# The second MLP of an attention and two-MLP kernel in five token chunks instead of six, with part of its weights streamed

## The chip, the cores and the metric

The kernel runs on one core of one Trainium2 chip. The metric is the device time of one execution in microseconds: before the change 1404.86 us, the median of 3 runs (1404.59 to 1405.29).

## The reference, cut to what matters

Attention (8 batches of 576 tokens, so 4608 tokens in all) gives 512 features per token, a gated MLP follows (hidden width 1536), and then the second MLP, which alone is touched here:

```
h = x @ w_in            # x 4608 x 512, w_in 512 x 2048
g = h * cos(h)
out = g @ w_out         # w_out 2048 x 512
```

All of it is float32. The kernel feeds TensorE with float32r operands, each number split into a high and a low part, and makes three passes (high by high, high by low, low by high) for every product.

## The kernel before, in words

The tokens of the second MLP are cut into chunks. A chunk has two halves of `TH` = 384 tokens, so that six chunks cover 4608. Both matrix products of a chunk are done by a Strassen-like scheme with seven products in place of eight; the halves are one of the directions that it cuts. Every matmul has a 128x128 weight tile as its stationary operand, and one half (384 columns) of one operand as its moving one.

*Up phase* (`period`, `product`). All six chunks go through the up product first. A chunk has eight periods (`NPF`, the pieces of the hidden width); a period makes the seven products of one piece, six matmuls each. The products are numbered by `n`; the order on TensorE in a period is 0 of this period, 3 and 4 of the one before, 1 of this one, 6 and 5 of the one before, 2 of this one. ScalarE copies sums between the PSUM tiles (`copy`), and with VectorE it makes the cosine of the period before (`phase`, `rest`, `sine`, `times`), which GpSimd's queue stores to `h2` in DRAM (`store_g`). `x_work` fits the next chunk in: its four quadrants `xb` are loaded, VectorE makes four sums `xt` of them, and each of the seven operands is split into high and low (`split_x2`: ScalarE writes the high part, VectorE the low one) into a tile `xs`. The tables `X_SUM`, `X_NEXT` and `X_THIS` say at which place of which period.

*Down phase* (`down_mm` and the loop at the end). Chunk after chunk, seven products of 48 matmuls each (`ORDER`); the operands are read back from `h2` (`load_g`, tiles `raw2`), combined by VectorE (`sums2`), split (`prep2`), and the results are evicted, transposed and stored (`evict2`, `finish_out`). The first chunk's operands are prepared in the last periods of the up phase (`PREP2`).

*Storage.* Weight pieces of 256 KB (`up`, `wd`) live in 56 slots (areas `U_AREAS`), which hold all 56 up pieces; as the last chunk's up products finish with them, the slots take 48 of the 56 down pieces (eight slots are left for partial sums). Only the down pieces of products 4 and 2 take turns in one set of slots (`RING`). The `xs` tiles have 9 buffers, the tiles called `x` (loads, sums, cosines) 16. A tile is taken when its code line is reached; the instruction that first writes it waits on the chip until the last reader of the slot's former tile is done.

*What sets the order.* The order on each engine is the one in which the code is written (a manual schedule); there is no planner. Loads go out on SyncE's queue (SP), which issues them in code order: a load whose slot is not free yet holds back every load behind it, but SP runs ahead of the other engines as far as slots allow.

Of the kernel before, what the change touches and what calls it, by code (L numbers as in the profile page):

```python
# [30 lines left out]
TH = 384  # L31
NCH = NT // (2 * TH)
# [11 lines left out]
U_AREAS = (6, 4, 4, 6, 6, 6, 2, 4, 4, 4, 4, 2, 2, 2)  # L44
U_FIRST = (0, 7, 4, 5, 11, 2, 8, 13, 9, 3, 10, 6, 12, 1)
RING = (4, 2)
# [20 lines left out]
def attention_mlp_kernel(ctx: ExitStack, tc: tile.TileContext, qT, kT, vP, pP, wgv, w12, out):  # L67
# [627 lines left out]
    def xt(shape, dt, name):  # L695
        if "m" in late:
            return lt(shape, dt, "x", name, 16)
        x_n[0] += 1
        if x_n[0] <= 4:
            return w2_new(shape, dt, "r" if x_n[0] <= 2 else "p", name)  # L700
        return hr_tile((0, 0) if x_n[0] <= 7 else (0, 1), shape, name)
# [3 lines left out]
    def load_x2(c):  # L705
        for a in range(2):
            for t in range(2):
                xb[a, t] = xt([128, 2, TH], F32, "xb")
                r0 = 2 * TH * c + TH * t
                SP.dma_start(out=xb[a, t], in_=x2d[2 * a:2 * a + 2, :, r0:r0 + TH].rearrange("k p n -> p k n"))  # L710

    def sum_x2(key, x, y):
        xb[key] = xt([128, 2, TH], F32, "xt")
        DVE.tensor_tensor(out=xb[key], in0=xb[x], in1=xb[y], op=ALU.subtract)
# [8 lines left out]
    def new_xs():  # L723
        return late["x"].tile([128, 2, 2, TH], F32R, tag="xs", name="xs", bufs=9)

    def split_x2(n, to):
        if to[n] is None:
            to[n] = new_xs()
        split(xb.pop(RIGHT[n]), to[n][:, 0], to[n][:, 1])

    with tc.manual_schedule():
# [145 lines left out]
        for s_ in range(len(SETS)):  # L877
            end = s_ == len(SETS) - 1
            for i in range(7):
                evict = strassen(s_, i)  # L880
                sums1(s_, i)
                for fp in range(3):
                    prep(*nxt(s_, i), fp)
                if i == 4:
                    load_h(s_ + 1, 0, 0)
                elif i == 5:
                    load_h(s_ + 1, 1, 1)
                    load_h(s_ + 1, 0, 1)
                elif i == 6:
                    load_h(s_ + 1, 1, 0)  # L890
                for _ in range(STEPS_D[s_][i]):
                    w2_step()
                if (s_, i) == (3, 6):
                    w2_flush()
                if end and i == 1:
                    load_x2(0)
                elif end and i == 4:
                    stage["gates"].close()
                    stage["pad"].close()
                    late["x"] = ctx.enter_context(tc.tile_pool(name="xs", bufs=1, side="right", reuse_waits="tile"))  # L900
                    x_now = [new_xs() for _ in range(7)]
# [27 lines left out]
        areas = [a for a in U_FIRST for _ in range(U_AREAS[a])]  # L929

        def load_up(q, n):
            a = tag_of["up", q, n] = areas.pop(0)
            up[q, n] = slots[a].pop(0)
# [5 lines left out]
        def load_wd(n, f):  # L939
# [3 lines left out]
        def vt():  # L943
            return lt([128, 2, TH], F32, "v", "v", 2)

        for q in range(3):
            for n in UP_ORDER:
                load_up(q, n)
# [11 lines left out]
        def bd_tiles():  # L960
            return [pu.tile([128, 512], F32, tag=n, name=n)[:, :TH] for n in ("pb", "pd")]
# [26 lines left out]
        def store_g(p, t, g):  # L988
            c, q = divmod(p, NPF)
            r0 = 2 * TH * c + TH * t  # L990
            nc.gpsimd.dma_start(out=h2[2 * q:2 * q + 2, :, r0:r0 + TH].rearrange("f p n -> p f n"), in_=g)
# [21 lines left out]
        def xt3(name):  # L1013
            return lt([128, 2, TH], F32, "x", name, 16)
# [26 lines left out]
        def down_mm(i, fps, ms_all=((0, 1),)):  # L1041
            n = ORDER[i]
            which = {0: 0, 1: 0, 3: 0, 4: 1, 6: 2, 2: 3, 5: 3}[n]
            first = n in (0, 4, 6, 2)
            if first and 0 in fps:
                if which == 3:
                    acc2[which] = bd_tiles()
                else:
                    o2 = ac_tile("o2")
                    acc2[which] = [o2[:, m, :TH] for m in range(2)]  # L1050
# [18 lines left out]
        def load_g(s_, k, t):  # L1069
            if s_ < NCH:  # L1070
                r0 = 2 * TH * s_ + TH * t
                for fp in range(4):
                    r = raw2[s_, k, t, fp] = xt3("raw2")
                    f0 = NPF * k + 2 * fp
                    SP.dma_start(out=r, in_=h2[f0:f0 + 2, :, r0:r0 + TH].rearrange("f p n -> p f n"))
# [4 lines left out]
        def prep2(s_, n, fp):  # L1080
# [3 lines left out]
            g = g2[n, fp] = new_xs()  # L1084
# [17 lines left out]
        def finish_out(s_, a, t, o_):  # L1102
            ot = lt([128, TH // 32, 2, 32], F32, "v", "ot", 2)
            for m in range(2):
                DVE.transpose(out=ot[:, :, m, :], in_=o_[m])  # L1105
            r0 = 2 * TH * s_ + TH * t
            queues = (nc.gpsimd,) if s_ < NCH - 1 else (SP, ACT) if (a, t) == (1, 0) else (SP,)
            for al in range(4):
                c0 = 128 * al + 64 * a
                queues[al % len(queues)].dma_start(  # L1110
                    out=out[r0:r0 + TH, c0:c0 + 64].rearrange("(b r) d -> r b d", r=32),
# [3 lines left out]
        def evict2(s_, n, acc):  # L1115
            for m in range(2):
                if n in (0, 1, 2, 3):
                    part2[n, m] = ut((n, m), [128, TH], F32, "part")
                    copy(part2[n, m], acc[m])
# [25 lines left out]
        def period(p):  # L1145
            new, old, older = (pairs.get(x) for x in (p, p - 1, p - 2))
            if p <= LAST:
                c, q = divmod(p, NPF)
                if p >= 1 and p + 2 < NPF:
                    for n in UP_ORDER:  # L1150
                        load_up(p + 2, n)
# [3 lines left out]

            def A(x):
                return x["ac"][:, 0, :TH]

            def C(x):
                return x["ac"][:, 1, :TH]  # L1160
# [8 lines left out]
            if older:  # L1169
                older["p"] = xt3("cp")  # L1170
                phase(older["p"], older["ac"][:, :, :TH])
            if p <= LAST and p != 1:
                start(p)
            if old and p != 1:
                product(D_, p - 1, 3, True)
            if p == 0:
                mark(B_, p)
                pairs[1] = {"ac": ac_tile("ac")}
                start(1)
            if p <= LAST:  # L1180
                copy(B_, A(new))
            if older:
                rest(older["p"], older["ac"][:, :, :TH])
                older["s"] = xt3("cs")
                phase(older["s"], older["hs"])
            if old:
                product(A(old), p - 1, 4, False)
                old["hs"] = xt3("hs")
                plus(old["hs"][:, 1], old["v"][:, 1], D_)
# [4 lines left out]
            if p <= LAST:  # L1194
                product(B_, p, 1, False)
            elif old:
                down_mm(0, (0,))
            if old:
                product(D_, p - 1, 6, False)
            if older:  # L1200
                times(older["p"], older["ac"][:, :, :TH])
                store_g(p - 2, 0, older.pop("p"))
                del older["ac"]
            if p <= LAST:
                copy(C(new), B_)
                new["v"] = vt()
                copy(new["v"][:, 0], B_)
            if older:
                sine(older["s"])
            if p > LAST and old:  # L1210
                down_mm(0, (1,))
            if old:
                product(C(old), p - 1, 5, False)
                plus(old["hs"][:, 0], old["v"][:, 0], D_)
# [6 lines left out]
            if p == 0:  # L1221
                product(D_, p, 3, True)
# [17 lines left out]
        for s_ in range(NCH):  # L1240
            for i in range(7):
                n = ORDER[i]
                acc = down_mm(
                    i, (2, 3) if s_ == i == 0 else range(4), ((0,), (1,)) if (s_, i) == (NCH - 1, 6) else ((0, 1),)
                )
                if n in RING:
                    for f in range(NPF):
                        del wd[n, f]
                        ut_done(("wd", n, f))
                    if n == RING[1] and s_ + 1 < NCH or n == RING[0]:  # L1250
                        for f in range(NPF):
                            load_wd(RING[1] if n == RING[0] else RING[0], f)
# [12 lines left out]
                elif i == 6:  # L1265
                    load_g(s_ + 1, 1, 0)
                if s_ or i != 1:
# [46 lines left out]
```

## Time and profile before

| | |
|---|---|
| median of 3 runs | 1404.86 us |
| profiled execution | 1405.46 us, span 1403.7 us |
| TensorE busy | 1387.8 us (99%) |
| VectorE busy | 1130.4 us (81%) |
| ScalarE busy | 829.8 us (59%) |
| DMA | 329.35 MB, mean 235 GB/s |
| the second MLP's matmuls | from 698.4 to 1399.1 us of the span |

PE is TensorE's matmuls, PEld its weight loads, DVE VectorE, ACT ScalarE, POOL GpSimd, SP SyncE; an engine with a q behind it is its DMA queue. The granted TensorE clock is at full speed in all 40 slices of the span. Matmuls are pipelined: the duration of one is longer than the distance from one to the next, and the distance is what the time is made of.

### The profile page before, as it was taken

The page shows a single profiled execution, that of the slowest core. Times are in us where ns is not written, and L with a number is a line of the kernel's source. Part 1 is how long each engine was busy: PE and PEld are TensorE (multiplying, and loading weights), DVE is VectorE, ACT ScalarE, POOL GpSimd, SP SyncE. Part 2 cuts the span into 40 slices and gives each one's busy share as a digit, 9 for nine tenths or more (in the row PEclk, how much of TensorE's full clock was granted, in tenths as well). Part 3 has the DMA queues.
Part 4 walks back from the last instruction along what each step waited for, and adds up shares of the span by engine and source line. Part 5 has one row for each costly group of instructions (what it writes and reads, how often), then busy time and mean ns, then how long its engine had stood idle before and what let it go on. Part 6 is the DMA issues. An engine that isn't in the chain of part 4 may idle for free.

```text
span 1403.7 us, 25278 instructions
## 1 busy us (share of the span) xinstructions
PE 1387.8 (99%) x9644; PEld 1278.5 (91%) x9644; DVE 1130.4 (81%) x1515; ACT 829.8 (59%) x1226; POOL 257.9 (18%) x424
## 2 busy tenths in 40 slices
PE   8999999999999999999999999999999999999998
PEld 6678888888898888898899999999999999999998
DVE  5779889889866898987858778787779788787886
ACT  5866566666644555554558777787775444544443
POOL 1112222222231111121012211212211202112020
PEclk9999999999999999999999999999999999999999
DMA  8947978887698648358494243242798756747641
GB/s 328 408 174 271 356 262 305 311 284 287 248 411 306 233 165 305 137 189 305 146 386 158 108 151 145 115 157 113 270 391 262 272 202 198 251 123 267 207 143 34
DMA packets 148504, 329.35 MB, mean 235 GB/s; under 512 B 21664, under 2 KB 58016, under 8 KB 146976
## 3 DMA queue, kind: packets, MB, share of 16 engines
q1 hardware_dynamic: 110240, 201.95, 41.1%
q0 software_dynamic: 36480, 123.76, 22.5%
q10 hardware_dynamic: 1664, 2.03, 0.4%
q8 instruction: 76, 1.25, 0.4%
q14 instruction: 44, 0.36, 0.1%
HBM read 202.38 MB, written 125.30 MB: 233 GB/s over the span
## 4 chain that ended last, share of the span: by engine, by line
PE 90%; DVE 4%; issue 2%; DMA 2%; ACT 1%; POOL 0%; POOLq 0%; ACTq 0%; SPq 0%; DVEq 0%
PE o L1057 18%; PE o L652 17%; PE ac L971 14%; PE pv L535 7%; PE pg L535 7%; PE pd L971 7%; PE pd L1057 4%; PE pb L1057 4%; PE pb L971 4%; PE wp L495 3%; PE pv L524 2%; PE pg L524 1%; DMA hr<-h 1%; PE pp L234 1%; PE tp L224 1%
## 5 line engine op out<-in xcount | busy, mean ns | idle before, releaser
L652 PE MATMUL o<-g,w 128*128 128x512 f32 (+1 forms) x1260 | 259.7, 368 | 2.2 <-DVE g L112 1.4
L652 PEld LDWEIGHTS o<-g,w 128*128 128x128 f32 x1260 | 219.3, 189 | 42.3 <-DVE g L112 1.9
L1057 PE MATMUL o<-xs,wd 128*128 128x384 f32 x1440 | 251.9, 336 | 0.0
L1057 PEld LDWEIGHTS o<-xs,wd 128*128 128x128 f32 x1440 | 249.8, 188 | 0.0
L971 PE MATMUL ac<-xs,up 128*128 128x384 f32 x1152 | 215.9, 336 | 0.6 <-ACT v L1008 0.6
L971 PEld LDWEIGHTS ac<-xs,up 128*128 128x128 f32 x1152 | 201.1, 188 | 1.0 <-ACT v L1008 0.9
L111 ACT ACTIVATE xs<-raw 128x768 fp32r<-128x768 f32 x168 | 134.0, 845 | 71.8 <-DVE raw L1100 69.0
L112 DVE TENSOR_TENSOR xs<-raw,xs 128x768 fp32r<-128x768 f32 x168 | 149.6, 950 | 23.6 <-ACT xs L111 23.6
L535 PE MATMUL pv<-a,wp 128*128 128x288 f32 x1008 | 150.6, 298 | 3.0 <-DVE h L567 2.8
L535 PEld LDWEIGHTS pg<-a,wp 128*128 128x128 f32 x1008 | 137.7, 188 | 16.8 <-issue 5.7
L111 ACT ACTIVATE g<-hr 128x1024 fp32r<-128x1024 f32 (+1 forms) x105 | 101.3, 977 | 85.1 <-DVE hr L632 34.7
L535 PE MATMUL pg<-a,wp 128*128 128x288 f32 x1008 | 150.3, 298 | 0.4 <-ACT E L208 0.4
L535 PEld LDWEIGHTS pv<-a,wp 128*128 128x128 f32 x1008 | 137.6, 188 | 11.5 <-DVE h L567 5.7
L112 DVE TENSOR_TENSOR g<-hr,g 128x1024 fp32r<-128x1024 f32 (+1 forms) x105 | 113.0, 1113 | 30.9 <-ACT g L111 30.8
L553 ACT ACTIVATE silu<-pg 128x576 f32<-128x576 f32 x96 | 62.5, 652 | 112.8 <-PE pg L535 103.9
L971 PE MATMUL pd<-xs,up 128*128 128x384 f32 x576 | 115.5, 336 | 0.0
L567 DVE TENSOR_TENSOR h<-silu,pv 128x576 f32<-128x576 f32 x96 | 72.1, 751 | 52.2 <-PE pv L535 18.2
L971 PEld LDWEIGHTS pd<-xs,up 128*128 128x128 f32 x576 | 101.0, 188 | 0.2
L568 POOL DMA_DIRECT2D h<-h x96 | 53.2, 554 | 243.3 <-DVE h L567 221.7
L1110 POOL DMA_DIRECT2D out<-ot x80 | 49.4, 620 | 242.5 <-DVE ot L1105 179.0
L1100 DVE TENSOR_TENSOR raw<-raw,raw 128x768 f32<-128x768 f32 x96 | 86.0, 949 | 1.0 <-DMA raw<-h 0.8
L997 DVE SCALAR_TENSOR_TENSOR cp<-ac,cp 128x768 f32<-128x768 f32 x48 | 45.9, 956 | 40.4 <-ACT cp L994 39.6
(132 smaller groups left out, 2070.2 us busy)
## 6 DMA issues: line engine op xcount, KB each, us to landing
raw<-h SPq DMA_DIRECT2D x96, 384.0 KB, 7.1
wd<-w2d SPq DMA_DIRECT2D x136, 256.0 KB, 5.7
h<-h POOLq DMA_DIRECT2D x96, 288.0 KB, 5.3
hr<-h SPq DMA_DIRECT2D x48, 512.0 KB, 7.2
raw<-in_w SPq DMA_DIRECT2D x44, 512.0 KB, 4.8
h<-cp POOLq DMA_DIRECT2D x48, 384.0 KB, 3.1
h<-cs POOLq DMA_DIRECT2D x48, 384.0 KB, 2.8
up<-w2u SPq DMA_DIRECT2D x56, 256.0 KB, 6.7
```

Source lines behind the costliest of these rows:

```text
L111: ACT.activation(out=hi, in_=src, func=AF.Copy)
L112: eng.tensor_tensor(out=lo, in0=src, in1=hi.bitcast(F32), op=ALU.subtract)
L535: PE.matmul(out=p_[:, c, :HS], lhsT=w[:, u, x, o:o + 128], rhs=a2[b][:, u, y, HS * c:HS * c + HS], start=(n == 0), stop=(n == 5),)
L553: ACT.activation(out=s_, in_=pg[:, :, :HS], func=AF.Silu)
L567: DVE.tensor_tensor(out=h_, in0=s_, in1=pv[:, :, :HS], op=ALU.mult)
L568: nc.gpsimd.dma_start(out=h1[f, :, S * b:S * b + S], in_=h_.rearrange("p c n -> p (c n)"))
L652: PE.matmul(out=acc[:, m, :N], lhsT=wd1[n, fp][:, j, 256 * x + 128 * m:256 * x + 128 * m + 128], rhs=g1[n, fp][:, y, j, :], start=(first a ...
L971: PE.matmul(out=out, lhsT=w[:, u, 128 * k:128 * k + 128], rhs=x[:, v, k, :], start=(first and k == 0 and i == 0), stop=(k == 1 and i == 2) ...
L997: DVE.scalar_tensor_tensor(out=out, in0=h_, scalar=1.0 / TWO_PI, in1=out.bitcast(I32), op0=ALU.mult, op1=ALU.subtract)
L1057: PE.matmul(out=acc[m], lhsT=wd[n, 2 * fp + j][:, x, 128 * m:128 * m + 128], rhs=g2[n, fp][:, y, j, :], start=(first and fp + j + q == 0), ...
L1100: DVE.tensor_tensor(out=to, in0=x, in1=y, op=ALU.subtract)
L1110: queues[al % len(queues)].dma_start(out=out[r0:r0 + TH, c0:c0 + 64].rearrange("(b r) d -> r b d", r=32), in_=ot[32 * al:32 * al + 32].rea ...
```

## The change: what it does

The half widths come from a table `TW` with one entry per chunk: two chunks with halves of 480 tokens and three of 448. Every place that had `TH` takes the chunk's width. Tiles have the width of the largest chunk (`xs`: 512), and to hold them 11 of the 56 weight slots go and one of the nine `xs` buffers.

With 45 weight slots, the up pieces of periods 0 to 4 stay resident (`QS` = 5, 35 slots), and the 21 pieces of periods 5 to 7 go through the other ten slots in every chunk. A product that is done with a streamed piece frees the slot and the next streamed piece is loaded (`up_ring`). In the down phase the pieces of products 4, 1, 3 and 5 are streamed (32 of 56 per chunk); 13 of them are loaded ahead of the first chunk. The loads of the down ring now stand behind the chunk's `load_g` calls, at the same place in the loop. The split of the second operand moves from place (6, 2) to (7, 0).

```diff
-TH = 384
-NCH = NT // (2 * TH)
+TW = (480, 480, 448, 448, 448)
+TX = max(TW)
+NCH = len(TW)
+T0 = tuple(2 * sum(TW[:c]) for c in range(NCH))
-RING = (4, 2)
+QS = 5
+RING = (4, 1, 3, 5)
...
-    def new_xs():
-        return late["x"].tile([128, 2, 2, TH], F32R, tag="xs", name="xs", bufs=9)
+    def new_xs(w):
+        return late["x"].tile([128, 2, 2, 512], F32R, tag="xs", name="xs", bufs=8)[:, :, :, :w]
...
+        up_first = [(q, n) for q in range(QS) for n in UP_ORDER]
+        up_ring = [
+            (q, n) for p in range(QS, NPF + 1)
+            for q, n in ((p, 0), (p - 1, 3), (p - 1, 4), (p, 1), (p - 1, 6), (p - 1, 5), (p, 2)) if QS <= q < NPF
+        ] * NCH
...
-        wd_first = [(n, f) for n in (0, 4, 6, 1, 3, 5) for f in range(NPF)]
+        wd_ring = [(n, f) for n in RING for f in range(NPF)] * NCH
+        wd_first = [(n, f) for n in (0, 4, 6, 1, 2) for f in range(NPF) if n not in RING]
+        ahead = sum(U_AREAS) - 8 - len(wd_first)
...
-            if c == NCH - 1:
+            if c == NCH - 1 or q >= QS:
                 del up[q, n]
                 ut_done(("up", q, n))
-                if wd_first:
-                    load_wd(*wd_first.pop(0))
+                if up_ring:
+                    load_up()
+                elif c == NCH - 1 and wd_first:
+                    load_wd()
...
-        X_NEXT = {(6, 0): (0,), (6, 2): (1,), (7, 1): (2,), (7, 2): (3,)}
+        X_NEXT = {(6, 0): (0,), (7, 0): (1,), (7, 1): (2,), (7, 2): (3,)}
...
-                if n in RING:
-                    for f in range(NPF):
-                        del wd[n, f]
-                        ut_done(("wd", n, f))
-                    if n == RING[1] and s_ + 1 < NCH or n == RING[0]:
-                        for f in range(NPF):
-                            load_wd(RING[1] if n == RING[0] else RING[0], f)
...
+                if n in RING:
+                    for f in range(NPF):
+                        del wd[n, f]
+                        ut_done(("wd", n, f))
+                        if wd_ring:
+                            load_wd()
```

On SP in the up phase the order before is this (`xb` are the quadrants of a chunk, `up` and `wd` weight pieces; the first row is the first chunk's load):

```order
L710 DMA xb<-x2d 128x2x384 x4
L934 DMA up<-w2u 128x512 x28
L710 DMA xb<-x2d 128x2x384 x4
L934 DMA up<-w2u 128x512 x28
L710 DMA xb<-x2d 128x2x384 x16
L941 DMA wd<-w2d 128x512 x10
```

and of the change, the same place of the same queue is this:

```order
L714 DMA xb<-x2d 128x2x480 x4
L948 DMA up<-w2u 128x512 x28
L714 DMA xb<-x2d 128x2x480 x4
L948 DMA up<-w2u 128x512 x38
L714 DMA xb<-x2d 128x2x448 x4
L948 DMA up<-w2u 128x512 x21
L714 DMA xb<-x2d 128x2x448 x4
L948 DMA up<-w2u 128x512 x21
L714 DMA xb<-x2d 128x2x448 x4
L948 DMA up<-w2u 128x512 x31
```

Before, the quadrants of the third to sixth chunk stood one behind the other; now 21 streamed weight loads of a chunk stand ahead of each.

On ACT at the end of a chunk's up phase, from its seventh period on, the order before is this (`xs<-xb` and `xs<-xt` are splits for the next chunk):

```order
L111 ACTIVATE xs<-xb 128x768
L1008 ACTIVATE ac<-pb 128x384
L1008 ACTIVATE v<-pb 128x384
L1002 ACTIVATE cs<-cs,half_pi 128x768
L111 ACTIVATE xs<-xt 128x768
L1008 ACTIVATE v<-ac 128x384
L994 ACTIVATE cp<-ac 128x768
```

and of the change this:

```order
L114 ACTIVATE xs<-xb 128x2x448
L1030 ACTIVATE ac<-pb 128x448
L1030 ACTIVATE v<-pb 128x448
L1024 ACTIVATE cs<-cs,half_pi 128x2x448
L1030 ACTIVATE v<-ac 128x448
L1016 ACTIVATE cp<-ac 128x2x448
L1030 ACTIVATE pb<-ac 128x448
L1016 ACTIVATE cs<-hs 128x2x448
L1024 ACTIVATE cp<-cp,half_pi 128x2x448
L114 ACTIVATE xs<-xt 128x2x448
```

The second split (`xs<-xt`) went from the end of the seventh period to the inside of the eighth, behind three copies and the cosine's steps of that period.

## Rows read from the trace of the kernel before

**Rows 1.** The page, busy time of each engine over the span.

```profile
span 1403.7 us, 25278 instructions
PE 1387.8 (99%) x9644; PEld 1278.5 (91%) x9644; DVE 1130.4 (81%) x1515; ACT 829.8 (59%) x1226; POOL 257.9 (18%) x424
```

**Rows 2.** Stages: window, its length, busy of each engine, clock, DMA share, GB/s.

```profile
core 0: us, PE busy (x) PEld busy (x) DVE busy (x) ACT busy (x) POOL busy (x), PEclk, DMA share, GB/s
...
805.00:863.00 58.00, 58.00 (x336) 57.95 (x335) 45.96 (x59) 43.92 (x71) 11.46 (x16) 1.00 0.36 136
...
980.00:1039.00 59.00, 59.00 (x342) 58.95 (x341) 42.05 (x54) 43.11 (x71) 12.17 (x17) 1.00 0.86 321
1039.00:1108.00 69.00, 69.00 (x400) 68.94 (x399) 61.59 (x78) 42.09 (x60) 8.02 (x12) 1.00 0.91 318
...
1224.00:1283.00 59.00, 59.00 (x342) 59.00 (x342) 46.14 (x60) 25.40 (x36) 9.86 (x16) 1.00 0.63 209
```

**Rows 3.** The chain of waits in order of time: start, length, what, count.

```profile
400.01 1.59 PE pv L535 x12
```

**Rows 4.** The chain at the start of the second MLP.

```profile
704.28 0.50 ACT v L1008
704.83 1.32 PE ac L971 x6
...
708.23 3.12 PE ac L971 x18
```

**Rows 5.** The chain in the first down chunk.

```profile
1053.74 29.12 PE o L1057 x168
1082.86 0.53 PE pb L1057 x3
...
1107.85 2.25 PE o L1057 x13
```

**Rows 6.** The timeline of PE where the first MLP ends: start, length, instruction, count.

```profile
675.69 22.83 PE L652 MATMUL o<-g,w 128*128 128x512 f32 x100
698.36 1.21 PE L971 MATMUL ac<-xs,up 128*128 128x384 f32 x6
```

**Rows 7.** VectorE by the timeline, operations of two widths.

```profile
680.61 1.23 DVE L112 TENSOR_TENSOR g<-hr,g 128x1024 fp32r<-128x1024 f32 x1 [1.49 <-ACT g L111]
681.75 0.95 DVE L714 TENSOR_TENSOR xt<-xb 128x768 f32<-128x768 f32 x1
```

**Rows 8.** ScalarE by the timeline, where one chunk's up periods end.

```profile
810.96 1.58 ACT L111 ACTIVATE xs<-xt 128x768 fp32r<-128x768 f32 x2
812.44 0.49 ACT L1008 ACTIVATE v<-ac 128x384 f32<-128x384 f32 x1
812.83 0.81 ACT L994 ACTIVATE cp<-ac 128x768 int32<-128x768 f32 x1
813.82 0.47 ACT L1008 ACTIVATE pb<-ac 128x384 f32<-128x384 f32 x1 [0.18 <-ACT cp L994]
```

**Rows 9.** TensorE there.

```profile
815.36 1.20 PE L971 MATMUL pb<-xs,up 128*128 128x384 f32 x6
```

**Rows 10.** DMA issues from 681 to 730 us: count, KB each, median us to landing.

```profile
up<-w2u SPq DMA_DIRECT2D x50, 256.0 KB, 6.9
```

**Rows 11.** DMA issues from 760 to 1040 us.

```profile
xb<-x2d SPq DMA_DIRECT2D x12, 384.0 KB, 3.6
```

**Rows 12.** VectorE by the timeline, first down chunk.

```profile
1065.52 7.54 DVE L1100 TENSOR_TENSOR raw<-raw,raw 128x768 f32<-128x768 f32 x8 [0.82 <-DMA raw<-h]
1072.97 3.56 DVE L112 TENSOR_TENSOR xs<-raw,xs 128x768 fp32r<-128x768 f32 x4
...
1081.78 7.03 DVE L112 TENSOR_TENSOR xs<-raw,xs 128x768 fp32r<-128x768 f32 x8
```

**Rows 13.** VectorE by the timeline at the end of the span.

```profile
1399.09 0.58 DVE L1105 STREAM_TRANSPOSE ot<-pd 128x384 f32<-128x384 f32 x1 [1.59 <-PE pd L1057]
```

More of the change, by code (lines that the diff above doesn't have):

```diff
@@ L693, in attention_mlp_kernel, with xt @@
     x_n = [0]
-    def xt(shape, dt, name):
+    def xt(name, w):
         if "m" in late:
-            return lt(shape, dt, "x", name, 16)
+            return lt([128, 2, TX], F32, "x", name, 16)[:, :, :w]
         x_n[0] += 1
         if x_n[0] <= 4:
-            return w2_new(shape, dt, "r" if x_n[0] <= 2 else "p", name)
-        return hr_tile((0, 0) if x_n[0] <= 7 else (0, 1), shape, name)
+            return w2_new([128, 2, w], F32, "r" if x_n[0] <= 2 else "p", name)
+        return hr_tile((0, 0) if x_n[0] <= 7 else (0, 1), [128, 2, w], name)
     xb, xs = {}, {}
@@ L707, in load_x2 @@
             for t in range(2):
-                xb[a, t] = xt([128, 2, TH], F32, "xb")
-                r0 = 2 * TH * c + TH * t
-                SP.dma_start(out=xb[a, t], in_=x2d[2 * a:2 * a + 2, :, r0:r0 + TH].rearrange("k p n -> p k n"))
+                w = TW[c]
+                xb[a, t] = xt("xb", w)
+                r0 = T0[c] + w * t
+                SP.dma_start(out=xb[a, t], in_=x2d[2 * a:2 * a + 2, :, r0:r0 + w].rearrange("k p n -> p k n"))
     def sum_x2(key, x, y):
-        xb[key] = xt([128, 2, TH], F32, "xt")
+        xb[key] = xt("xt", xb[x].shape[2])
         DVE.tensor_tensor(out=xb[key], in0=xb[x], in1=xb[y], op=ALU.subtract)
@@ L721, in sums_x2 @@
             del xb[0, 1]
-    def new_xs():
-        return late["x"].tile([128, 2, 2, TH], F32R, tag="xs", name="xs", bufs=9)
+    def new_xs(w):
+        return late["x"].tile([128, 2, 2, 512], F32R, tag="xs", name="xs", bufs=8)[:, :, :, :w]
     def split_x2(n, to):
+        x = xb.pop(RIGHT[n])
         if to[n] is None:
-            to[n] = new_xs()
-        split(xb.pop(RIGHT[n]), to[n][:, 0], to[n][:, 1])
+            to[n] = new_xs(x.shape[2])
+        split(x, to[n][:, 0], to[n][:, 1])
     with tc.manual_schedule():
@@ L900, in attention_mlp_kernel @@
                     late["x"] = ctx.enter_context(tc.tile_pool(name="xs", bufs=1, side="right", reuse_waits="tile"))
-                    x_now = [new_xs() for _ in range(7)]
+                    x_now = [new_xs(TW[0]) for _ in range(7)]
                     late["x"].tile([128, 128], F32, name="late_pad")
@@ L929, in attention_mlp_kernel, with load_up, load_wd, vt @@
         areas = [a for a in U_FIRST for _ in range(U_AREAS[a])]
-        def load_up(q, n):
-            a = tag_of["up", q, n] = areas.pop(0)
-            up[q, n] = slots[a].pop(0)
+        up_first = [(q, n) for q in range(QS) for n in UP_ORDER]
[3 more added lines that the diff above has]
+        ] * NCH
+        def load_up():
+            q, n = (up_first or up_ring).pop(0)
+            if areas:
+                a = tag_of["up", q, n] = areas.pop(0)
+                up[q, n] = slots[a].pop(0)
+            else:
+                up[q, n] = ut(("up", q, n), [128, 2, 256], F32R, "up")
             SP.dma_start(out=up[q, n].bitcast(F32).rearrange("p x c -> p (x c)"), in_=w2u[q, PIECE[n]])
         wd = {}
-        wd_first = [(n, f) for n in (0, 4, 6, 1, 3, 5) for f in range(NPF)]
-        def load_wd(n, f):
+        wd_ring = [(n, f) for n in RING for f in range(NPF)] * NCH
+        wd_first = [(n, f) for n in (0, 4, 6, 1, 2) for f in range(NPF) if n not in RING]
+        ahead = sum(U_AREAS) - 8 - len(wd_first)
+        for k, (n, f) in enumerate(wd_ring[:ahead]):
+            wd_first.insert((8 if n == 4 else 16) + k, (n, f))
+        del wd_ring[:ahead]
+        def load_wd():
+            n, f = (wd_first or wd_ring).pop(0)
             wd[n, f] = ut(("wd", n, f), [128, 2, 256], F32R, "wd")
             SP.dma_start(out=wd[n, f].bitcast(F32).rearrange("p x c -> p (x c)"), in_=w2d[f, PIECE[n]])
[L943 to L948, printed above, removed]
+        def vt(w):
+            return lt([128, 2, TX], F32, "v", "v", 2)[:, :, :w]
+        for _ in range(21):
+            load_up()
         xs_of = {0: x_now}
@@ L960, in bd_tiles @@
         def bd_tiles():
-            return [pu.tile([128, 512], F32, tag=n, name=n)[:, :TH] for n in ("pb", "pd")]
+            return [pu.tile([128, 512], F32, tag=n, name=n) for n in ("pb", "pd")]
         B_, D_ = bd_tiles()
@@ L989, in store_g @@
             c, q = divmod(p, NPF)
-            r0 = 2 * TH * c + TH * t
-            nc.gpsimd.dma_start(out=h2[2 * q:2 * q + 2, :, r0:r0 + TH].rearrange("f p n -> p f n"), in_=g)
+            w = TW[c]
+            r0 = T0[c] + w * t
+            nc.gpsimd.dma_start(out=h2[2 * q:2 * q + 2, :, r0:r0 + w].rearrange("f p n -> p f n"), in_=g)
         def phase(out, h_):
@@ L1046, in down_mm @@
                 if which == 3:
-                    acc2[which] = bd_tiles()
+                    acc2[which] = [x[:, :w] for x in bd_tiles()]
                 else:
                     o2 = ac_tile("o2")
-                    acc2[which] = [o2[:, m, :TH] for m in range(2)]
+                    acc2[which] = [o2[:, m, :w] for m in range(2)]
             acc = acc2[which]
@@ L1117, in evict2 @@
                 if n in (0, 1, 2, 3):
-                    part2[n, m] = ut((n, m), [128, TH], F32, "part")
+                    part2[n, m] = ut((n, m), [128, TX], F32, "part")[:, :TW[s_]]
                     copy(part2[n, m], acc[m])
@@ L1148, in period @@
                 c, q = divmod(p, NPF)
-                if p >= 1 and p + 2 < NPF:
-                    for n in UP_ORDER:
-                        load_up(p + 2, n)
+                if p >= 1:
+                    for _ in range(min(7, len(areas))):
+                        load_up()
                 if p != 1:
@@ L1154, in period @@
                 new = pairs[p]
+            w, v, u = (TW[x // NPF] if 0 <= x <= LAST else 0 for x in (p, p - 1, p - 2))
             def A(x):
-                return x["ac"][:, 0, :TH]
+                return x["ac"][:, 0, :v if x is old else w]
             def C(x):
-                return x["ac"][:, 1, :TH]
+                return x["ac"][:, 1, :v if x is old else w]
             def start(p):
@@ L1169, in period @@
             if older:
-                older["p"] = xt3("cp")
-                phase(older["p"], older["ac"][:, :, :TH])
+                older["p"] = xt("cp", u)
+                phase(older["p"], older["ac"][:, :, :u])
             if p <= LAST and p != 1:
@@ L1174, in period @@
             if old and p != 1:
-                product(D_, p - 1, 3, True)
+                product(D_[:, :v], p - 1, 3, True)
             if p == 0:
-                mark(B_, p)
+                mark(B_[:, :w], p)
                 pairs[1] = {"ac": ac_tile("ac")}
@@ L1180, in period @@
             if p <= LAST:
-                copy(B_, A(new))
+                copy(B_[:, :w], A(new))
             if older:
-                rest(older["p"], older["ac"][:, :, :TH])
-                older["s"] = xt3("cs")
+                rest(older["p"], older["ac"][:, :, :u])
+                older["s"] = xt("cs", u)
                 phase(older["s"], older["hs"])
@@ L1187, in period @@
                 product(A(old), p - 1, 4, False)
[L1188 to L1189 removed]
+                old["hs"] = xt("hs", v)
+                plus(old["hs"][:, 1], old["v"][:, 1], D_[:, :v])
             if older:
@@ L1194, in period @@
             if p <= LAST:
-                product(B_, p, 1, False)
+                product(B_[:, :w], p, 1, False)
             elif old:
-                down_mm(0, (0,))
+                down_mm(0, 0, (0,))
             if old:
-                product(D_, p - 1, 6, False)
+                product(D_[:, :v], p - 1, 6, False)
             if older:
-                times(older["p"], older["ac"][:, :, :TH])
+                times(older["p"], older["ac"][:, :, :u])
                 store_g(p - 2, 0, older.pop("p"))
@@ L1204, in period @@
             if p <= LAST:
-                copy(C(new), B_)
-                new["v"] = vt()
-                copy(new["v"][:, 0], B_)
+                copy(C(new), B_[:, :w])
+                new["v"] = vt(w)
+                copy(new["v"][:, 0], B_[:, :w])
             if older:
@@ L1221, in period @@
             if p == 0:
-                product(D_, p, 3, True)
+                product(D_[:, :w], p, 3, True)
             if p <= LAST:
@@ L1243, in attention_mlp_kernel @@
                 acc = down_mm(
-                    i, (2, 3) if s_ == i == 0 else range(4), ((0,), (1,)) if (s_, i) == (NCH - 1, 6) else ((0, 1),)
+                    s_, i, (2, 3) if s_ == i == 0 else range(4), ((0,), (1,)) if (s_, i) == (NCH - 1, 6) else ((0, 1),)
                 )
-                if n in RING:
-                    for f in range(NPF):
-                        del wd[n, f]
-                        ut_done(("wd", n, f))
-                    if n == RING[1] and s_ + 1 < NCH or n == RING[0]:
-                        for f in range(NPF):
-                            load_wd(RING[1] if n == RING[0] else RING[0], f)
                 if i not in (1, 4):
```

31 lines of the change are left out of this document (16 added, 15 removed).

## The prediction

> **What bounds the kernel now.** I read the page's busy times first: TensorE 99% of the span, VectorE 81%, ScalarE 59% [rows 1]. Then the stages: in an up chunk (805 to 863 us) and in a down chunk (1224 to 1283 us) TensorE is busy for all of the window, 58.00 of 58.00 and 59.00 of 59.00, at full clock; it is so too in the two windows in which the up phase hands over to the down phase (980 to 1108 us), where the DMA share is 0.86 and 0.91 [rows 2]. VectorE is at 46 of 58 us in the steady stages and 61.6 of 69 in the hand-over. The chain of waits says the same: from the start of the second MLP it is TensorE, piece after piece, with one wait of 0.50 us for a ScalarE copy [rows 4], and the end [rows 13]. So the time of the second MLP is the number of its matmuls times the distance between two, and all else matters only where it becomes late.
>
> **The matmuls.** A chunk has 7 x 8 x 6 = 336 in the up phase and 7 x 48 = 336 in the down phase, 672 whatever its width. Six chunks make 4032, five 3360. The columns in all stay the same (4608 tokens), so what goes is the part of a matmul's distance that doesn't grow with its columns. The rows give it at three widths, at one column per cycle of 2.4 GHz:
> - 288 columns: 1.59 us for 12, 132.5 ns each, 120.0 of it columns, 12.5 over [rows 3].
> - 384 columns: 3.12 us for 18, 173.3 ns, 160.0 of it columns, 13.3 over [rows 4].
> - 512 columns: 100 from 675.69 to 698.36, 226.7 ns, 213.3 of it columns, 13.4 over [rows 6].
>
> The widths 448 and 480 aren't in the trace; they lie between the rows of 384 and 512, so I take 200.0 and 213.4 ns. Before: 4032 x 173.3 = 698.9 us. After: two chunks of 480, 1344 x 213.4 = 286.8; three of 448, 2016 x 200.0 = 403.2; together 690.0. Difference -8.9 us. With the 12.5 of the row at 288 it would be -11.7; if a width of 480 were paced like the next row, 512, the sum would be 304.7 + 403.2 = 707.9, +9.0. The row at 288 speaks against such steps: that width is no multiple of 64 or 128, and it pays for its own columns.
>
> In "TensorE: Matmul & The Clock Gate", the Trainium skill (section "Wait — 56ns, not 53.3ns?") gives about 2.5 ns over the columns for back-to-back matmuls. By that, the 672 matmuls that go would save 1.7 us and no more. The rows of this case have 12.5 to 13.4 at every width, with weights of their own for every matmul, so I go by them.
>
> **What stays beside TensorE.** VectorE and ScalarE get the same elements in fewer, longer instructions. VectorE takes 0.95 us for 768 elements and 1.23 for 1024 [rows 7], so about 1.16 for 960: 1.22 times, where a matmul gets 213.4 / 173.3 = 1.23 times longer. Their cover is the same in proportion, and they stay at nothing. The two-row access of 2 x 480 elements in place of 768 in one run costs nothing visible either: the cosine's first step already reads two separate halves and takes 0.81 us [rows 8].
>
> *Up weights, streamed.* Each product of periods 5 to 7 waits for a load that was issued when the streamed piece ten places before it was done with. At least nine products stand between, 9 x 6 x 200 = 10.8 us. A 256 KB load lands 6.9 us after its issue in the worst stretch, the first burst of 50 [rows 10]. In the up chunks the DMA share is 0.36 [rows 2]; 21 loads of 0.26 MB in three periods of 8.4 us add 218 GB/s to 136, 354 in all, where the burst stages move 321. 10.8 against 6.9: hidden, cost 0, but the closest of the streams.
>
> *The quadrants of the next chunk* now stand on SP behind the 21 streamed loads, the last of which waits for a product one period into the next chunk. They land in 3.6 us [rows 11], and their first sum stands two periods (17 us) further on. Cost 0.
>
> *Down weights, streamed.* A ring piece takes a slot that was freed three to five products before its use, some 28 us or more at 9.6 us a product. A chunk's bytes become, at 448, 16 x 0.459 + 32 x 0.262 + 1.84 = 17.6 MB in 67.2 us, 261 GB/s in place of 209, below the 318 at which TensorE already runs full [rows 2]. Cost 0.
>
> *Eight `xs` buffers, and the moved split.* At a chunk's end the fourth split's slot now comes free with the last product of period 7, not with an earlier one, so ScalarE makes it after that and not before. Two splits took 1.58 us [rows 8]; one, 0.8, stands ahead of the three instructions of the next period, the last of which (`pb<-ac`, 813.82 + 0.47 = 814.29) is waited for by the product at 815.36 [rows 9]. Cover 1.07, of which 0.8 is used, 0.3 left (0.3 at the new widths too). Cost 0; if ScalarE is later than that, up to 0.8 us at each of four borders, 3 us.
>
> *The first down chunk* has the least cover. There the sums begin when the last `raw` loads land, 1065.52, 11.78 after TensorE is through with the up products (1053.74), and the first low part that product 2 needs is done at 1081.78 + 0.95 = 1082.73 [rows 12]. TensorE starts that product at 1082.86 and reads the low part with its second matmul, at 1083.03 [rows 5]: 0.3 us to spare. After: TensorE needs it at 168 x 213.4 = 35.9 + 0.2 = 36.1 us after that point; VectorE has its 17.2 us of work times 1.22 = 21.0 after loads that land at 11.8 to 14.7 (one to 1.25 times), so 32.8 to 35.7. Cost 0, with 0.4 to 3.3 to spare.
>
> *Both ends.* The copy behind the one wait [rows 4] has 480 columns for 384: +0.1. After the last matmul a transpose (0.58 us [rows 13]) and the stores of a block with 1.17 times the bytes: +0.3 of the 4.6 us from there to the span's end.
>
> **The sum.** -8.9 + 0.4 = -8.5 us, against the profiled execution of 1405.46 (span 1403.7) 1396.96. The median of the runs is 0.6 lower, so 1396.4.
>
> **Rivals.**
> 1. *Part of it is eaten at the hand-overs.* For it: 0.3 us of cover in the first down chunk, 0.3 left at four borders, DMA shares near 0.9. Against it: cover grows with the matmuls. If the loads of the first down chunk come 3 us later than 1.25 times, TensorE waits for about 2.6; the borders add up to 3. Time 1397.5 to 1402, 1400 as its middle.
> 2. *The part that is not columns grows with them.* It could come from the weight load beside each matmul, or from waits between them, and stretch with the width: the distances would be 173.3 x 480/384 = 216.7 and 202.2 ns, and 3360 of them again make 698.9 us. Then nothing goes, and the ends cost 0.4: 1405.3. Against it: 12.5, 13.3 and 13.4 at three widths. By the Trainium skill's 2.5 ns (the page and section named above) the time would be 1404.86 - 1.7 + 0.4 = 1403.6, on the same side of the 0.2%.
> 3. *The streamed up weights come late: slower.* Ten slots give 10.8 us. Were a landing L longer than that, TensorE would wait L - 10.8 about twice per chunk, ten times in all. From L = 11.65 the gain is gone, from 11.9 the kernel is slower by 0.2%; at 12.5 it takes 1396.4 + 17 = 1413. Against it: 6.9 in the fullest burst.
> 4. *480 columns are paced as 512*: +9.0 + 0.4, 1414.3. Against it: the row at 288.
>
> **How the numbers follow.** The forecast has 77 in 100, rival 1 has 11, rival 2 and whatever else leaves the time as it was 5, rival 3 has 5, rival 4 has 2. About 0.2% (2.8 us) is what a measurement of this kernel can tell from no change. Faster by more than that are the forecast and rival 1: 0.88. The same: 0.05. Slower: 0.07. The range goes from 1395.0 (a little of the way to the -11.7 of the row at 288) to 1401.0, which takes in most of rival 1.
>
> **What would show it.** In the chain, 18 up matmuls in 3.84 us (480) and 3.60 (448), 192 down matmuls in 41.0 and 38.4; an up chunk in 71.7 and 67.2 us with TensorE busy throughout. Rival 1 shows as a wait of TensorE for a low part in the first down chunk or for `pb<-ac` at a chunk's first period; rival 3 as waits for DMA `up` in the last three periods of each up chunk, with landings over 10 us; rivals 2 and 4 as another distance between matmuls with no wait at all. The prediction is wrong where TensorE has more than 1 us of idle time in the second MLP, or where the distances aren't 200 and 213 ns.

## The result, and the profile after

The changed kernel takes 1416.49 us, median of four runs (1415.07 to 1417.66), the kernel before on the same chip 1404.97: a ratio of 1.0082, 95% interval 1.0064 to 1.0099. It is slower by 0.8%; 1396.4 was predicted. Between the profiled executions, 1415.07 and 1405.46, the difference is 9.6 us.

The page of the changed kernel, the lines that answer to [rows 1]:

```profile
span 1413.3 us, 23896 instructions
PE 1396.3 (99%) x8972; PEld 1209.3 (86%) x8972; DVE 1123.8 (80%) x1396; ACT 818.2 (58%) x1119; POOL 239.3 (17%) x392
```

TensorE has 672 matmuls fewer, as the change says, and is busy for 8.5 us more. Is it kept waiting? Four windows of the stages (columns as in [rows 2]), and the waits of TensorE from 698 us to the end:

```profile
760.00:840.00 80.00, 80.00 (x366) 68.24 (x365) 61.30 (x64) 58.34 (x79) 11.86 (x17) 1.00 0.62 216
974.00:1045.00 71.00, 71.00 (x349) 65.14 (x348) 51.27 (x57) 51.34 (x74) 11.50 (x16) 1.00 1.00 372
1045.00:1120.00 75.00, 75.00 (x346) 64.58 (x345) 64.62 (x66) 40.78 (x50) 6.99 (x10) 1.00 0.84 276
1190.00:1260.00 70.00, 70.00 (x340) 63.45 (x339) 53.43 (x60) 29.21 (x36) 10.52 (x16) 1.00 0.75 252
```

```profile
PE ac L990 <- ACT v L1030: 0.7, 1, 0.7
```

It isn't: TensorE is full in every window, at full clock, even where the DMA share is 1.00, and the one wait is that of [rows 4], 0.7 us where the kernel before waits 0.6. So the distance from one matmul to the next is longer. The chain of waits has them (start, length, what, count): up matmuls of 480 columns, up of 448, down of 448, and the end.

```profile
705.94 0.58 ACT v L1030
...
710.79 3.96 PE ac L990 x18
...
883.86 3.68 PE ac L990 x18
...
1388.66 9.81 PE o L1076 x48
...
1403.38 4.92 PE pd L1076 x24
1408.32 0.65 DVE ot L1126
```

3.96 / 18 is 220.0 ns, where 213.4 was taken; 3.68 / 18 and 9.81 / 48 are 204.4, for 200.0. The second MLP's matmuls then cost 1344 x 220.0 + 2016 x 204.4 = 707.8 us against 698.9 before: +8.9. From the last matmul (1408.30) to the end of the span it is 5.0 us, where it was 4.6. These two are 9.3 of the 9.6 us. In cycles of 2.4 GHz a matmul of 480 pays 48 over its columns and one of 448 some 43; the 384 and 512 columns of the kernel before pay 32 [rows 4, 6].

### The profile page after: what moved, and what is told of

It is laid out like the page before. It is cut to its first block, busy times and chain, and to the rows that moved or that the text cites. A ratio compares the mean times of both kernels' runs of the same rounds, so it can differ in the third digit from the quotient of the medians.

```text
span 1413.3 us, 23896 instructions
## 1 busy us (share of the span) xinstructions
PE 1396.3 (99%) x8972; PEld 1209.3 (86%) x8972; DVE 1123.8 (80%) x1396; ACT 818.2 (58%) x1119; POOL 239.3 (17%) x392
## 4 chain that ended last, share of the span: by engine, by line
PE 89%; DVE 4%; issue 3%; DMA 2%; ACT 1%; POOL 0%; SPq 0%; ACTq 0%; POOLq 0%; DVEq 0%
PE o L1076 18%; PE o L655 16%; PE ac L990 14%; PE pv L538 7%; PE pd L990 7%; PE pg L538 7%; PE pb L1076 4%; PE pb L990 4%; PE pd L1076 4%; PE wp L498 2%; PE pv L527 2%; PE pg L527 1%; PE pp L237 1%; DVE h L570 1%; PE tp L227 1%
## 5 line engine op out<-in xcount | busy, mean ns | idle before, releaser
L1076 PE MATMUL o<-xs,wd 128*128 128x448 f32 (+1 forms) x1200 | 254.7, 373 | 0.0
L1076 PEld LDWEIGHTS o<-xs,wd 128*128 128x128 f32 x1200 | 225.2, 188 | 27.6
L990 PE MATMUL ac<-xs,up 128*128 128x448 f32 (+1 forms) x960 | 215.7, 373 | 0.7 <-ACT v L1030 0.7
L990 PEld LDWEIGHTS ac<-xs,up 128*128 128x128 f32 x960 | 180.0, 188 | 23.2 <-ACT v L1030 1.1
L114 ACT ACTIVATE xs<-raw 128x896 fp32r<-128x896 f32 (+1 forms) x140 | 130.7, 973 | 82.0 <-DVE raw L1120 67.5
L115 DVE TENSOR_TENSOR xs<-raw,xs 128x896 fp32r<-128x896 f32 (+1 forms) x140 | 147.2, 1110 | 21.9 <-ACT xs L114 21.8
L990 PE MATMUL pd<-xs,up 128*128 128x448 f32 (+1 forms) x480 | 114.0, 373 | 0.0
L990 PEld LDWEIGHTS pd<-xs,up 128*128 128x128 f32 x480 | 90.1, 188 | 11.0
L1120 DVE TENSOR_TENSOR raw<-raw,raw 128x896 f32<-128x896 f32 (+1 forms) x80 | 84.5, 1109 | 0.1
L1019 DVE SCALAR_TENSOR_TENSOR cp<-ac,cp 128x896 f32<-128x896 f32 (+1 forms) x40 | 44.7, 1117 | 48.7 <-ACT cp L1016 48.7
```

Of the source, the lines that this page charges most:

```text
L114: ACT.activation(out=hi, in_=src, func=AF.Copy)
L115: eng.tensor_tensor(out=lo, in0=src, in1=hi.bitcast(F32), op=ALU.subtract)
L990: PE.matmul(out=out, lhsT=w[:, u, 128 * k:128 * k + 128], rhs=x[:, v, k, :], start=(first and k == 0 and i == 0), stop=(k == 1 and i == 2) ...
L1019: DVE.scalar_tensor_tensor(out=out, in0=h_, scalar=1.0 / TWO_PI, in1=out.bitcast(I32), op0=ALU.mult, op1=ALU.subtract)
L1076: PE.matmul(out=acc[m], lhsT=wd[n, 2 * fp + j][:, x, 128 * m:128 * m + 128], rhs=g2[n, fp][:, y, j, :], start=(first and fp + j + q == 0), ...
L1120: DVE.tensor_tensor(out=to, in0=x, in1=y, op=ALU.subtract)
```

## The experiments

Three causes could stand behind the distances: the width itself (W), the layout of the moving tiles (L), which the change set on rows 512 apart, or what runs beside (S). Later theories took over from L: the address at which the moving rows begin (A), or that address against the one of the weights (R).

**Streams of nothing but matmuls, by width.** The edit: a kernel of its own, each stream one line.

> A kernel with nothing but streams of 60 matmuls each (three passes, own weights for each, as in the second MLP); it computes none of the reference. Nineteen widths with the four rows of a tile close together, then 384, 416, 448 and 480 with rows 512 apart as in the changed kernel, 448 and 480 from an offset of 16 elements, and 384, 448, 480 with the same weights again and again. Theory W (the width itself): 480 has 220.0 ns and 448 has 204.5 in every layout, 384 has 173.3 and 512 has 226.7, and the other widths show which widths are dear. Theory L (the layout: rows 512 apart): 480 has 213.4 and 448 has 200.0 with close rows, and 220.0 and 204.5 only with rows 512 apart; 384 with rows 512 apart is above 173.3. Theory S (what runs beside: streams, VectorE, ScalarE): 213.4 and 200.0 everywhere here.

Its chain of waits: 384, 448, 480 and 512 columns with rows close together (L70, L82, L88, L94), 448 and 480 with rows 512 apart (L103, L106), 448 from 16 elements on (L127).

```profile
75.49 10.43 PE acc L70 x60
...
120.00 12.39 PE acc L82 x60
...
144.94 13.09 PE acc L88 x60
...
171.44 13.62 PE acc L94 x60
...
206.78 12.39 PE acc L103 x60
219.17 13.00 PE acc L106 x60
...
308.44 12.00 PE acc L127 x60
```

173.8, 206.5, 218.2 and 227.0 ns; with rows 512 apart 206.5 and 216.7. Nothing ran beside, so S falls, and close rows aren't cheaper, so L falls. But W doesn't stand alone: 448 columns that begin 64 bytes later take 200.0, the predicted distance. With close rows from the tile's start, all widths up to 384 that were tried pay 29 to 33 cycles over their columns, those from 400 to 504 pay 37 to 48, and 512 pays 33. At most of these widths the four close rows of a tile begin at different places against the weights, so this list mixes width and address; with rows 512 apart, all at one place, 416, 448 and 480 columns pay 36, 48 and 40. The three streams that load the same weights again for every matmul take 173.5, 206.5 and 218.3 ns (384, 448, 480), so it makes no difference here whether the weights change.

**Rows close together in the kernel.**

```diff
-        return late["x"].tile([128, 2, 2, 512], F32R, tag="xs", name="xs", bufs=8)[:, :, :, :w]
+        x = late["x"].tile([128, 2048], F32R, tag="xs", name="xs", bufs=8)
+        return x[:, :4 * w].rearrange("p (v k n) -> p v k n", v=2, k=2)
```

> The changed kernel with the rows of every xs tile one width apart, in place of 512. Theory W: no change, 1416.5 us, distances 220.0 and 204.5 ns. Theory L: distances 213.4 and 200.0, 3360 matmuls give back 17.9 us, 1398 to 1399. Theory S: 1416.5.

1413.32 us (ratio 1.0062, 1.0046 to 1.0079). 448 columns stay at 3.68 us for 18; 480 come to 3.92 (217.8 ns) in the up phase and to 10.52 for 48 (219.2) in the down phase. The layout is worth some 3 us, not 18: L is out, and what little moved did so with rows that now begin at other addresses.

**The streams alone, at 384.**

```diff
-TW = (480, 480, 448, 448, 448)
+TW = (384,) * 6
```

> The streams, the eight xs buffers of rows 512 apart and the moved split of the changed kernel, but six chunks of 384 as before. Theory W: 173.3 ns and 1405 us, the time before. Theory L and theory S: more than 173.3 ns; with the same share as at 480 (220.0 for 213.4, 3 in 100) 4032 matmuls of 178.7, some 22 us more, 1426; at the least the 11 and 16 cycles of 448 and 480, 4.5 to 6.6 ns each, 1423 to 1431.

1408.76 us (1.0026, 1.0016 to 1.0036), by none of the theories. The matmuls are at 173.3 ns, but TensorE waits at the borders of the down chunks, 2.6 us in all. VectorE and then GpSimd at the first border, by the timeline (start, length, instruction, in brackets the idle time before and what ended it):

```profile
1102.84 3.52 DVE L115 TENSOR_TENSOR xs<-raw,xs 128x768 fp32r<-128x768 f32 x4
1114.24 0.58 DVE L1126 STREAM_TRANSPOSE ot<-pb 128x384 f32<-128x384 f32 x1 [7.88 <-DMA out<-ot]
1114.75 0.54 DVE L1126 STREAM_TRANSPOSE ot<-pd 128x384 f32<-128x384 f32 x1
1115.21 3.52 DVE L115 TENSOR_TENSOR xs<-raw,xs 128x768 fp32r<-128x768 f32 x4
```

```profile
1101.47 1.23 POOL L1131 DMA_DIRECT2D out<-ot  x2 [18.32 <-DVE ot L1126]
1108.17 1.23 POOL L1131 DMA_DIRECT2D out<-ot  x2 [5.46 <-issue]
1113.34 0.62 POOL L1131 DMA_DIRECT2D out<-ot  x1 [3.94 <-issue]
```

GpSimd puts out two stores and then none for 5.5 us. A transpose needs the tile that they empty (`ot` has two buffers), so it stands in VectorE's queue for 7.9 us, and behind it the low parts that TensorE wants: it waits until 1116.18, 0.97 after 1115.21.

**Widths whose distances the trace before shows.**

```diff
-TW = (480, 480, 448, 448, 448)
-U_AREAS = (6, 4, 4, 6, 6, 6, 2, 4, 4, 3)
-U_FIRST = (0, 7, 4, 5, 2, 8, 9, 3, 6, 1)
-QS = 5
+TW = (512, 512, 512, 384, 384)
+U_AREAS = (6, 4, 4, 6, 6, 6, 2, 4, 4)
+U_FIRST = (0, 7, 4, 5, 2, 8, 3, 6, 1)
+QS = 4
```

> Five chunks again, of half widths 512, 512, 512, 384, 384: 4608 tokens in all and the same 3360 matmuls, but only widths whose distance the trace before shows. Three up slots fewer, so four up groups are resident and 28 pieces a chunk streamed. Theory W: 2016 x 226.7 + 1344 x 173.3 = 689.9 us in place of 698.9, so about 1396 to 1397. Theory L (rows 512 apart are close rows at 512, but not at 384): 1344 matmuls of 384 cost 5 ns more, 1403. Theory S: streams still there, 1405 or more.

1419.14 us (1.0106, 1.0091 to 1.0121): a miss for W and L (S had only a lower end, 1405), and the run that told most. 512 columns take 226.6 ns in the first MLP of this same trace (80 from 679.69 to 697.82), 233.3 in the second (18 in 4.20 us), and 6.4 us go at four borders:

```profile
679.69 18.30 PE L655 MATMUL o<-g,w 128*128 128x512 f32 x80
697.82 0.40 PE L990 MATMUL ac<-xs,up 128*128 128x512 f32 x1
```

```profile
887.46 4.20 PE ac L990 x18
```

```profile
PE o L1076 <- DVE xs L115: 6.4, 4, 2.9
```

One width with two distances in one execution: it is something about where the operands are. By the addresses in the compiled program the moving tiles of the first MLP begin 256 bytes after a multiple of 512 and so do all weights; the `xs` tiles, which lie against the other end of SBUF, begin 480 after one, in the kernel before too.

**Streams by start address.**

> Streams of 48 matmuls each and nothing else; none of the reference is computed. Widths 384, 448, 480 and 512; the moving rows begin 0, 32, 64, 128, 256 or 480 bytes after a multiple of 512 B (rows 2048 B apart), the weights 256 bytes after one as in the second MLP; then 480 and 512 with the weights at 0, 32 and 128, 512 from 480 with the weights at 0 and 480, and 416, 464, 496 from 0. Theory A (the address of the moving rows, in the second MLP 480 bytes after a multiple of 512): 512 has 226.7 ns from 0, 64, 128, 256, and 232 to 235 from 480 and from 32; 384 has 173.3 from everywhere; 480 and 448 have less than 220.0 and 204.5 from some of the starts. Theory W (the width alone): one distance per width, whatever the start. Theory R (weights and rows in one relation): the distance of 512 changes with the weights' start as much as with the rows'.

The chain, each row 48 matmuls: first 512 columns from 0, 32, 64, 128, 256 and 480 with the weights at 256 (L104 to L119), then from 0 with the weights at 0, 32 and 128 (L131 to L137), then from 480 with the weights at 0 and at 480 (L140, L143).

```profile
209.02 10.90 PE acc L104 x48
219.92 11.20 PE acc L107 x48
231.12 11.00 PE acc L110 x48
242.12 11.16 PE acc L113 x48
253.28 10.93 PE acc L116 x48
264.21 11.20 PE acc L119 x48
...
306.77 10.91 PE acc L131 x48
317.68 11.19 PE acc L134 x48
328.87 11.16 PE acc L137 x48
340.03 11.19 PE acc L140 x48
351.22 10.89 PE acc L143 x48
```

The same from the other rows of that chain, divided by 48, in ns (weights at 256):

```
rows begin at     0      32      64     128     256     480
384 columns   173.8   173.3   173.3   175.8   173.3   173.8
448 columns   202.7   206.5   200.0   204.0   206.5   204.4
480 columns   216.7   217.7   218.3   217.9   216.9   220.0
512 columns   227.1   233.3   229.2   232.5   227.7   233.3
```

At 512 it is R: rows at 480 are dear with weights at 256 or 0 and cheap (226.9) with weights at 480; rows at 0 are cheap with weights at 256 or 0 and dear with weights at 32 or 128. Cheap is a difference of a multiple of 256 bytes; A, by which the rows' start alone counts, falls with it. The column for 480 has the changed kernel's own two distances, 204.4 and 220.0. 384 columns are dear at one start only. 480 columns have 216.7 at best, so no placement that was tried gives the 213.4. R isn't the whole rule: 448 has 202.7 and 206.5 at two starts a multiple of 256 from the weights, and 480 columns from 0 with the weights at 128 took 10.56 us (220.0), from 128 with the weights at 256 only 217.9.

**The changed kernel, xs tiles begun 256 bytes after a multiple of 512.**

```diff
-                    late["x"].tile([128, 128], F32, name="late_pad")
+                    late["x"].tile([128, 184], F32, name="late_pad")
```

> The changed kernel with the xs tiles begun 256 bytes after a multiple of 512 B (a pad of 224 B more on that side), where they begin 480 after one; nothing else differs. Theory A: the distances of 480 and 448 fall below 220.0 and 204.5; at 218.5 and 204 about 1413, at the predicted 213.4 and 200.0 1398. Theory W: no change, 1416.

1416.35 us (1.0076, 1.0063 to 1.0089). No gain, and not by W: 480 columns fall to 3.90 us for 18 (216.7 ns) and 448 rise to 3.72 (206.7), as in the table's column for 256. 1344 x 3.3 less and 2016 x 2.3 more cancel, to 0.2 us.

**The 512 kernel with that pad, and with it and a larger descriptor space.**

```diff
-    nc = _bacc.Bacc("TRN2", target_bir_lowering=False, num_devices=1, dynamic_dma_scratch_size=1024)
+    nc = _bacc.Bacc("TRN2", target_bir_lowering=False, num_devices=1, dynamic_dma_scratch_size=2048)
```

> The kernel of half widths 512, 512, 512, 384, 384 with the xs tiles begun 256 bytes after a multiple of 512 B, as the moving tiles of the first MLP are, whose 512 columns take 226.7 ns. Theory A: 226.7 in place of 231 to 235, 2016 x 6.5 = 13 us less, 1406; the waits at the borders of the down chunks (some 8 us) stay. Theory W or S: 1419 as without the shift.

> The same, with twice the descriptor space for GpSimd's DMA queue (2048 B in place of 1024). In the trace of the 512 kernel the stores of the output tiles go out in pairs, each pair when the one before has landed, and a transpose that needs such a tile holds VectorE's queue for up to 12 us at a border. If that space is what pairs them, four go out at once, the transposes come 6 us earlier and the border waits go: 1396 to 1399. If not, as without it: 1406 by theory A.

With the pad alone 1412.10 us (1.0050, 1.0037 to 1.0062), where A had 1406. 512 columns are at 226.7 (4.08 us for 18), 13.3 us less, but the border waits grow from 6.4 to 9.7, and behind the longer ones TensorE runs at the lower of its clock levels, 1.2 GHz, for a while: after a wait of 2.57 us the granted clock is 0.63 in the 4.6 us that follow, then 1.00. These two windows:

```profile
1217.40:1222.00 4.60, 4.60 (x14) 3.61 (x14) 4.60 (x5) 2.03 (x3) 1.31 (x2) 0.63 0.35 89
1222.00:1226.00 4.00, 4.00 (x19) 3.34 (x18) 4.00 (x4) 0.00 (x0) 0.66 (x1) 1.00 0.78 213
```

With the larger space 1401.26 us (0.9975, 0.9965 to 0.9985): all border waits are gone, and the kernel is faster than both. (At 512 the stores had gone out one at a time, not in pairs.) It misses the 1396 to 1399 by a wait in the first MLP. TensorE's waits from 600 us on:

```profile
PE o L655 <- ACT g L114: 2.5, 1, 2.5
PE o L655 <- DVE g L115: 1.4, 2, 0.8
PE ac L990 <- ACT v L1030: 0.7, 1, 0.7
```

The kernel before has 0.8 us in the first of these; here it is 2.5, and the clock is down (0.59) for 4.2 us behind it, of which TensorE is busy for 3.4. By estimate that is 1.7 us of wait and 1.4 of slower matmuls, some 3 us together.

**The best starts for 480 and 448.** On top of the pad:

```diff
+        o = 16 if w == 448 else 0
-        return late["x"].tile([128, 2, 2, 512], F32R, tag="xs", name="xs", bufs=8)[:, :, :, :w]
+        return late["x"].tile([128, 2, 2, 512], F32R, tag="xs", name="xs", bufs=8)[:, :, :, o:o + w]
```

> The changed kernel at its own widths, with the moving rows where the streams were shortest: 480 from the weights' own place (both 256 bytes after a multiple of 512), 448 from 64 bytes further on. Theory R (the distance goes by the width and by how far the rows begin after the weights, modulo 256 B): 1344 x 216.7 + 2016 x 200.0 = 694.4 us in place of 707.9, so 1402 to 1403.5, on the other side of the kernel before. Theory W (the width alone): 1416.

1401.46 us (0.9980, 0.9971 to 0.9989), half a microsecond below R's range: 15 us less than the changed kernel by nothing but 224 and 64 bytes of padding. Its chain, 480 and then 448:

```profile
783.32 3.90 PE ac L991 x18
...
880.53 3.60 PE ac L991 x18
```

216.7 and 200.0 ns, 1344 x 216.7 + 2016 x 200.0 = 694.4 us.

**The streams at 384 with the larger space.** The edit is that of the descriptor space above, on the kernel of six chunks.

> Six chunks of 384 with the streams of the changed kernel, which took 1408.8, and twice the descriptor space for GpSimd's DMA queue. If the streams cost only through the paired stores that hold VectorE at the borders of the down chunks, those waits go and it takes 1404.5 to 1406, as before. If the streams cost in another way (late weights, landings), 1408 to 1409.

1405.66 us (1.0010, 1.0001 to 1.0019). At the same border GpSimd now puts out five stores at once, and the transpose waits 2.98 us instead of 7.88 (third line: the kernel before, 4.01):

```profile
1102.53 3.06 POOL L1131 DMA_DIRECT2D out<-ot  x5 [21.17 <-DVE ot L1126]
```

```profile
1110.40 0.58 DVE L1126 STREAM_TRANSPOSE ot<-pb 128x384 f32<-128x384 f32 x1 [2.98 <-DMA out<-ot]
```

```profile
1111.37 0.58 DVE L1105 STREAM_TRANSPOSE ot<-pb 128x384 f32<-128x384 f32 x1 [4.01 <-DMA out<-ot]
```

TensorE has no border wait left. Of the 3.9 us that the streams cost at 384, 3.1 went through these stores; what the other 0.8 are isn't shown, and the larger space was not tried on the kernel before.

**The narrow chunk first.**

```diff
-TW = (512, 512, 512, 384, 384)
+TW = (384, 512, 512, 512, 384)
```

> Half widths 384, 512, 512, 512, 384, rows from the weights' place, twice the descriptor space. Against the order 512, 512, 512, 384, 384 (1401.3) the tokens loaded for the first chunk are as in the kernel before, so that the wait of 2.5 us and the slow matmuls behind it near the end of the first MLP go back to 0.8: 1396.5 to 1398. If that wait doesn't come from those loads: 1401.

1402.19 us (1398.56 to 1406.33; ratio 0.9981, 0.9971 to 0.9991), not the 1396.5 to 1398. In this order the kernel leaves out part of the sums: by the code, the marks of the first three periods cover only the first chunk's 384 columns. The wait near the end of the first MLP is 2.2 us in its trace, so in that trace a smaller first chunk didn't take it away. Its cause stays open: the same wait is 0.8 us in the trace of 512 columns without the larger space, and 0.6 in that of 384 columns with it.

**The kernel before, 96 bytes further.**

```diff
-                    late["x"].tile([128, 128], F32, name="late_pad")
+                    late["x"].tile([128, 152], F32, name="late_pad")
```

> The kernel before with a pad of 96 B more beside the xs tiles, so that they begin 384 bytes after a multiple of 512 B (128 away from the weights, modulo 256) in place of 480; nothing else differs. Theory R: 175.9 ns in place of 173.3, 4032 x 2.6 = 10.5 us more, 1415.4. Theory W: 1404.9.

1415.23 us (1.0074, 1.0059 to 1.0089), with 18 matmuls of 384 in 3.17 us for the 3.12 of [rows 4]:

```profile
884.62 3.17 PE ac L971 x18
```

A pad that no instruction reads makes the kernel before 10 us slower. R had 1415.4. This is the effect of the address by itself, with no other edit.

## Why the prediction was wrong

- *The step that failed* is "The widths 448 and 480 aren't in the trace; they lie between the rows of 384 and 512, so I take 200.0 and 213.4 ns." They don't lie on the line between: even the best starts that were tried leave 480 columns at 216.7. The rows at 384 [rows 4] and 512 [rows 6] both come from places where the operands' addresses cost nothing: 384 columns are dear at one start only of the six tried, and the 512 of the first MLP had rows and weights at the same place. In the second MLP the rows lie 480 and the weights 256 bytes after a multiple of 512, and there 448, 480 and also 512 pay 11 to 16 cycles more. The term of -8.9 us is +8.9.
- *"The row at 288 speaks against such steps"* failed with it. In the streams the widths from 256 to 352 pay 29 to 32 cycles, also those whose rows begin at several places against the weights; a row in that range says nothing on 448 and 480.
- *Rival 4* was of the right kind (another distance with no wait) and had 2 in 100. Its 1414.3 is near by chance: 480 columns aren't paced as 512 (220.0, not 226.7), and 448 columns, which it left at 200.0, bring half of the loss.
- *Rivals 1 and 3 didn't happen.* TensorE has one wait, the one it had before. Up weights, quadrants, down weights, moved split and first down chunk cost nothing, as worked out.
- *One cover was not looked at.* The stores of the output tiles through GpSimd's queue hold VectorE at each border. With 480 columns they end in time. With the same streams at 384 the kernel lost 3.9 us, and 0.8 with the larger space. The prediction had called the up weights the closest of the streams.
- *Both ends* were right: +0.4 us from the last matmul to the end of the span, +0.1 at the head.
- *The reasoning behind the sum holds where the distances do.* With 216.7 and 200.0 ns it gives 694.4 - 698.9 + 0.4 = -4.1 us; measured, -3.4.

## What to carry to other kernels

A matmul's distance read at two widths is not a line through all widths: in these runs, with a weight load for every matmul, it depended at over 384 columns on the width and on where the moving rows begin against the weights, by up to 16 cycles, and a full TensorE with no wait showed it only as length over count. Before widths are changed, time a stream at the new width with the operands where the kernel will have them, and try a few pads; here they were worth 15 us. Where a store frees a tile that a busy engine needs next, look how many stores its queue has out at once.

## What the runs showed of the hardware that was not expected

- The distance of 512 columns is 226.7 to 227.7 ns with rows and weights a multiple of 256 bytes apart, and 229.2 to 233.3 at the other differences tried; 384 columns have 173.3 to 173.8, and 175.8 at a difference of 128. Why is open: the runs show which addresses are dear, not what is shared there.
- No stream of 400 to 504 columns that was tried came below 36 cycles over its columns, but for 448 from 64 bytes after the weights' place (32).
- With 1024 B of descriptor space GpSimd had one or two stores of an output tile out at once; with 2048 B it put out five in a row (three at 512 columns).
- After waits of 2.5 us TensorE's granted clock was 0.59 to 0.63 in the next 4 to 5 us; after waits of 0.6 and 0.7 us at the start of the second MLP, in the kernel before and the changed one, it was 1.00.
